# Delta rule and hard-swish MLP: the next step's product with the state moved into the run of the state update

## The chip, the cores and the metric

The kernel runs on one NeuronCore of a Trainium2 chip. A core has five engines that run side by side, each with its own queue of instructions: TensorE (PE, with its weight loads shown as PEld), VectorE (DVE), ScalarE (ACT), GpSimd (POOL) and SyncE (SP, which here only issues transfers). They wait for each other by semaphores. The metric is the device time of one execution in microseconds (us); less is better.

## The reference, cut to what matters

```python
batch, n_heads, seq, head_dim = (4, 8, 768, 48)
for t in range(S):
    kt, vt, bt = (k_n[:, :, t], v[:, :, t], beta[:, :, t, None])
    y[:, :, t] = np.einsum('bhd,bhde->bhe', q[:, :, t], state)
    v_old = np.einsum('bhde,bhd->bhe', state, kt)
    state = state + bt[:, :, :, None] * np.einsum('bhd,bhe->bhde', kt, vt - v_old)
...
h = x @ w_in
relu6 = np.clip(h + 3.0, 0.0, 6.0)
g = h * relu6 / 6.0
return (g @ w_out).astype(np.float32)
```

The first part is linear attention by the delta rule over 768 tokens for each of 4 x 8 heads of width 48; `k_n` are the keys divided by their norm. Its output, 3072 tokens by 384, goes through an MLP with 2048 hidden columns. All is float32.

## The kernel before

**Steps.** The 768 tokens are cut into 24 chunks of C = 32. One step t handles one chunk of all four batches and eight heads at once (4 x 32 = 128 partitions). Within a chunk the recurrence is turned into products of small matrices:

- `sc` (L547): keys times keys and queries times keys of the chunk, one 32x32 block a head. Masked and scaled by beta (L558) they become L, which is inverted, and LB.
- `X`: the inverse of the unit triangular matrix of L, made on VectorE for a group of four steps at a time (`inverse`, L759 and L764: 30 pairs of a product and a subtraction; L469 and L473 transpose into and out of the layout for it).
- `ks` (L806): keys and queries of the chunk times the state of the step before. Half of it, even and odd batches apart, gives R = V - K state (L901, L909); the other half starts the output y (ScalarE L843, VectorE L819).
- `pz` (L827): X R, copied by ScalarE to Z (L927).
- `su` (L938): the state's change, keys times Z, subtracted from the state by two VectorE operations of 128x384 (L956).
- `py` (L827): LB ("B") times Z, added to y (L863). y is then transposed on TensorE (`yt`, L873) and copied into the MLP's input `xT` (L877).

All of ks, pz, su, py and sc consist of 32 matmuls on 32- or 64-row tiles of TensorE (64 instructions each in the profile, as a float32 matmul is two). The keys and queries of a later step are transposed by four large matmuls each (`pt`, L524).

**MLP.** It works on blocks of two steps (256 tokens). From block 3 on the first product is formed by `up_by_eleven` (L1066: pairs `begin(j)`, `end(j)`; ScalarE copies, GpSimd adds L1030, VectorE L1093, L1097 and L1113 follow each end). From block 2 on the second product is formed by `down_by_seven` (L1226: seven products in two halves each, with sums of g on VectorE, L1212, ahead of some).

**Order.** The whole program is written out by hand; each engine runs its instructions in the program's order. The string ORDER gives the order up to step 4. From step LS = 5 on the main loop (L1469 and below) does it: each step has NU = 15 units, and in each unit one entry of `plan` is taken first (parts of the attention), then one unit of the MLP, then some of `fill` (VectorE's work on norms and inverses of a later group). `chain(t)`, `prep(t)` and `norms(g)` are generators; `take` runs one to its next `yield`. Before, `chain(t)` is taken in units 0 (ks), 1 and 2 (R), 3 (the y half), 4 (pz), 8 (su and py), 9 (y add and state update) and 10 (yt). A block's 14 half products down fall in units 13, 14 of an even step and 0 to 11 of the next; the 16 parts up follow.

**PSUM.** ks, su and sc share two pairs of banks (`ring("pc", 2, ...)`): ks and su take both pairs, sc one. The rest share four banks (`pm`).

**Fill.** `CHAIN` and `USED` are by unit and by form the time that VectorE is taken to be used by others; `due` spreads the inverse's 62 parts over what is left. The inverse of group g+1 starts at unit 6 of the second step of group g, and what is left is drained at unit 2 of the first step of group g+1.

Of the kernel before, what the change touches and what calls it, by code (L numbers as in the profile page):

```python
# [44 lines left out]
def kernel(  # L45
# [21 lines left out]
    nc = tc.nc  # L67
# [7 lines left out]
    GS = 4  # L75
# [696 lines left out]
        yield  # L772


    xTs, outs, zs = {}, {}, {}

    def banks(name, t, i):
        ring("pc", NPC, (name, t, i))
# [8 lines left out]
    def chain(t, whole=True):  # L787
# [7 lines left out]
            needs(("state", t - 1))  # L795
        bkb = bkb_of(t)

        def of_state():
            ph = [banks("ks", t, i) for i in range(2)]
            for p in range(NP):  # L800
                for b in (0, 2, 1, 3):
                    for e in range(2):
                        r = slice(DP * e, DP * e + DP)
                        c = slice(2 * C * (b // 2), 2 * C * (b // 2) + 2 * C)
                        y = b % 2
                        nc.tensor.matmul(  # L806
                            ph[y][c, e, D * p : D * p + D],
                            lhsT=KQ[r, p * B // 2 + b // 2, 2 * y : 2 * y + 2, :].rearrange(
                                "k y c -> k (y c)"
                            ),  # L810
                            rhs=state[r, b, p, :],
                            start=(p == 0), stop=True, skip_group_check=True,
                            tile_position=(DP * e, 2 * C * (b // 2)),
                        )
            return [pairs(x) for x in ph]
# [21 lines left out]
        def output(Z=None):  # L837

            if t > 0:
                needs(("turned", t - 1))  # L840
            y = work.tile([P, DM], FP32, name="y", bufs=1)
            if t > 0:
                nc.scalar.activation(  # L843
                    out=by_pair(y[:]), in_=even, func=ACTF.Copy, scale=parity[:, 1, 1:2]
                )
                past.add(("even", t))
                if ("R", t) in past:
                    read(("ks", t, 0))
                yield 1
                plus(y[:], odd, parity[:, 0, 1:2], y[:])  # L850
                read(*(("ks", t, i) for i in range(2)))
                yield
            needs(("Z", t))
            Z = zs.pop(t)
            ring("pm", NPM, ("py", t))
            py = psM.tile([P, 512], FP32, name="py", tag=slot["pm"])
            of_heads(py, lambda b: b ^ 1, lambda h: LB[:, he(h), :], Z)
            past.add(("BZ", t))
            yield
            if t == 0:  # L860
                nc.scalar.activation(out=y[:], in_=py[:, 0:DM], func=ACTF.Copy)
            else:
                nc.vector.tensor_tensor(out=y[:], in0=y[:], in1=py[:, 0:DM], op=ALU.add)  # L863
            read(("py", t))
            yield
            blk, cc = divmod(t, CB)
            if cc == 0:
                needs(*([("up", blk - 2)] if blk >= 2 else []))
                xTs[blk] = work.tile([128, NKT, TB], FP32, name="xT")
            ring("pm", NPM, ("yt", t))  # L870
            pt = psM.tile([128, NKT, P], FP32, name="yt", tag=slot["pm"])
            for s in range(NKT):
                nc.tensor.transpose(pt[:, s, :], y[:, s * 128 : (s + 1) * 128], ident[:])  # L873
            past.add(("turned", t))
            yield 1
            read(("yt", t))
            nc.scalar.activation(  # L877
                out=xTs[blk][:, :, cc * P : (cc + 1) * P], in_=pt[:], func=ACTF.Copy
            )
            past.add(("seam", t))  # L880
            yield
# [10 lines left out]
        if t == 0:  # L892
            R = vfl
        else:
            needs("parity")
            needs(("BZ", t - 1), ("su", t - 1))
            Rt = work.tile([P, DM], FP32, name="R", bufs=1)
            R = Rt[:]
            Rp = R.rearrange("p (e z) -> p e z", e=2)
            for e in range(2):  # L900
                nc.vector.scalar_tensor_tensor(  # L901
                    out=Rp[:, e].rearrange("p (a w) -> p a w", w=D), in0=even[:, e],
                    scalar=parity[:, 0, 0:1], in1=by_pair(vfl)[:, e], op0=ALU.mult, op1=ALU.add,
                )
            if ("even", t) in past:
                read(("ks", t, 0))
            if whole:
                yield
            nc.vector.scalar_tensor_tensor(  # L909
                out=Rp, in0=odd.rearrange("p e a w -> p e (a w)"), scalar=parity[:, 1, 0:1],  # L910
                in1=Rp, op0=ALU.mult, op1=ALU.add,
            )
            yield

        if whole and t > 0:
# [32 lines left out]
        past.add(("su", t))  # L948
        if whole:
            take(outs[t])  # L950
        yield
        if whole:
            take(outs[t])
        for i, x in enumerate(su):
            sv = state[:, 2 * i : 2 * i + 2].rearrange("p b a w -> p b (a w)")
            nc.vector.tensor_tensor(  # L956
# [2 lines left out]
        past.add(("state", t))  # L959
        read(*(("su", t, i) for i in range(B // 2)))  # L960
        yield
        if whole:
            take(outs[t])
            yield

# [395 lines left out]
    def chain_of(t):  # L1361
        return made(("h", t), lambda: chain(t))
# [53 lines left out]
        }  # L1416

    def behind_tensor(ins):
        last = next(
            i for i in reversed(nc.cur_bb.bb.instructions) if i.engine == mybir.EngineType.PE  # L1420
        )
        tc.add_manual_dep(
            ins, last.name,
            mybir.DependencyInfo(mybir.DependencyClass.Sync, mybir.DependencyReason.DATA),
            reason="held back",
        )

    def do(word):
        if word in ("K", "Q", "V", "W"):
# [22 lines left out]
    with tc.manual_schedule():  # L1452
# [11 lines left out]
        loads = iter(())  # L1464
        left = due = 0
        USED = {"up": 0.42, "eleven": 1.0, "down": 0.7}
        APART = (8, 12)
        CHAIN = {0: 0.45, 1: 0.75, 2: 0.75, 3: 0.4, 4: 0.4, 6: 0.5, 9: 0.8, 10: 0.6, 14: 0.2}
        for t in range(LS, N):  # L1469
            g, i = group(t)  # L1470
            ch = chain_of(t)
            behind = t == LS
            now, more, third, later = (prep_of(t + LA - n) for n in (2, 1, 0, -1))
            if not behind:
                now = third
            take(gens["v"], 4)
            if i == 0:
                left += 1
            if i == 2:
                loads = keys_of(g + 3)  # L1480
            plan = {
                0: lambda: take(ch),
                1: lambda: (take(ch), take(now)),
                2: lambda: (take(ch), take(now), take(gens["q"], 4)),
                3: lambda: take(ch),
                4: lambda: (take(ch), take(now, t not in APART)),
                5: lambda: take(now, t not in APART),
                6: lambda: take(now),
                7: lambda: take(now, t in APART),
                8: lambda: take(ch),  # L1490
                9: lambda: take(ch),
                10: lambda: take(ch),
                11: lambda: token_sums(t // CB),
                13: lambda: take(later),
            }
            if behind:
                plan[13] = None
                for u, gen in zip((3, 5, 5, 6, 7, 9, 10, 11, 12, 13), (more,) * 5 + (third,) * 5):
                    plan[u] = lambda old=plan.get(u), gen=gen: (old and old(), take(gen))
            ready = (1, 6)  # L1500
            for u in range(NU):
                if plan.get(u):
                    plan[u]()
                take(loads, 2)
                if (i, u) == (0, 2):
                    drain(fill)
                    left = 0
                    fill = norms_of(g + 2)
                if (i, u) == ready:
                    drain(fill)  # L1510
                    fill = inverse_of(g + 1)
                    take(fill)
                    left, due = 2 * (C - 2) + 2, 0.0
                take(rest)
                take(gens["a"])
                take(units)
                settle(1)
                while evicts:
                    evicts.pop(0)()
                if i == 1 == ready[0] and 5 < u < 7:  # L1520
                    continue
                if i == 0 or not left:
                    take(fill, 2 if i or u < 2 else u > 4)
                    continue
                room = max(1.65 - USED[mode["of"]] - CHAIN.get(u, 0), 0.15) / mode["mean"]
                due += room * left / max((GS - i) * NU - u, 1)
                due = min(due, 2.6)
                take(fill, int(due))
                left, due = max(left - int(due), 0), due - int(due)
            if behind:  # L1530
                take(later)
            drain(ch)
# [32 lines left out]
```

## Time and profile before

| | |
|---|---|
| time, median of 3 runs | 664.62 us (662.32 to 664.71) |
| span of the profiled execution, first to last instruction | 660.3 us |
| mean granted TensorE clock in it | 0.997 |
| L1066 PE, ph, busy | 156.8 us in 128x128 and 128x256 with `xT`, 55.9 with `beta_tok` |
| L1226 PE, po, busy | 110.6 + 86.7 us |
| L806 PE, ks | 26.9 us busy, 1472 instructions |
| L938 PE, su | 19.5 us busy, 1408 instructions |
| L1212 / L1113 DVE | 56.1 / 52.6 us busy |
| L759 / L764 DVE, inverse | 57.3 / 55.1 us busy, 150 each |

The time of a run is that of the whole execution; the span of the profiled one leaves out what lies ahead of the first and behind the last instruction. Busy times of small matmuls overlap on TensorE, so their sum is not time; what counts is from one's start to the next one's start.

### The profile page before, as it was taken

The page shows a single profiled execution, that of the slowest core. Times are in us where ns is not written, and L with a number is a line of the kernel's source. Part 1 is how long each engine was busy: PE and PEld are TensorE (multiplying, and loading weights), DVE is VectorE, ACT ScalarE, POOL GpSimd, SP SyncE. Part 2 cuts the span into 40 slices and gives each one's busy share as a digit, 9 for nine tenths or more (in the row PEclk, how much of TensorE's full clock was granted, in tenths as well). Part 3 has the DMA queues.
Part 4 walks back from the last instruction along what each step waited for, and adds up shares of the span by engine and source line. Part 5 has one row for each costly group of instructions (what it writes and reads, how often), then busy time and mean ns, then how long its engine had stood idle before and what let it go on. Part 6 is the DMA issues. An engine that isn't in the chain of part 4 may idle for free.

```text
span 660.3 us, 26640 instructions
## 1 busy us (share of the span) xinstructions
PE 632.5 (96%) x11640; PEld 569.2 (86%) x11640; DVE 499.2 (76%) x1170; ACT 282.3 (43%) x548; POOL 225.1 (34%) x352
## 2 busy tenths in 40 slices
PE   2768999999999999999999999999999999999997
PEld 2658987776689989999999999999999999999997
DVE  5899877798657988758988848979658998456354
ACT  5887689332243154154154244244244144153250
POOL 6531022003661353553254354164051242331430
PEclk9998999999999999999999999999999999999999
DMA  7888346202040030041030030020020020000000
GB/s 174 204 198 235 77 102 164 51 25 43 9 87 18 3 74 3 3 90 22 3 74 3 2 74 3 2 63 2 3 50 2 3 49 3 23 18 2 26 1 24
DMA packets 88692, 33.28 MB, mean 50 GB/s; under 512 B 80224, under 2 KB 83424, under 8 KB 88576
## 3 DMA queue, kind: packets, MB, share of 16 engines
q1 hardware_dynamic: 88224, 31.29, 20.8%
q8 instruction: 91, 1.49, 0.9%
q10 hardware_dynamic: 352, 0.30, 0.2%
q14 instruction: 25, 0.20, 0.1%
HBM read 26.84 MB, written 4.72 MB: 48 GB/s over the span
## 4 chain that ended last, share of the span: by engine, by line
PE 91%; DVE 3%; DMA 2%; SPq 1%; ACT 1%; issue 1%; DVEq 0%
PE po L1226 28%; PE ph L1066 27%; PE ph L994 9%; PE po L1162 6%; PE ks L806 4%; PE su L938 3%; PE pt L524 3%; PE pz L827 3%; PE py L827 3%; PE sc L547 2%; PE yt L873 1%; DMA spare<-in_moe_w_in_dram 1%; PE pi L684 1%; DMA w_out<-in_moe_w_in_dram 1%; SPq L168 1%
## 5 line engine op out<-in xcount | busy, mean ns | idle before, releaser
L1066 PE MATMUL ph<-xT,w_in 128*128 128x128 f32 (+1 forms) x720 | 156.8, 321 | 0.0
L1030 POOL TENSOR_TENSOR g<-g 128x256 f32<-128x256 f32 (+1 forms) x144 | 88.6, 616 | 104.7 <-ACT g L1080 99.1
L1066 PEld LDWEIGHTS ph<-xT,w_in 128*128 128x128 f32 x720 | 116.8, 191 | 6.7
L1226 PE MATMUL po<-w_out,g 128*128 128x192 f32 x640 | 110.6, 326 | 0.0
L1226 PEld LDWEIGHTS po<-w_out,g 128*128 128x128 f32 x640 | 104.6, 190 | 0.5
L1080 ACT ACTIVATE g<-ph 128x512 f32<-128x512 f32 x72 | 43.1, 598 | 105.1 <-PE ph L1066 105.1
L1226 PE MATMUL po<-spare,g 128*128 128x192 f32 x480 | 86.7, 332 | 0.0
L1226 PEld LDWEIGHTS po<-spare,g 128*128 128x128 f32 x480 | 77.2, 190 | 1.8
L994 PE MATMUL ph<-xT,w_in 128*128 128x128 f32 (+1 forms) x384 | 72.0, 338 | 0.6 <-ACT xT L877 0.6
L1236 POOL TENSOR_TENSOR o<-o,u 128x192 f32<-128x192 f32 x18 | 13.3, 739 | 163.8 <-ACT o L1233 86.6
L994 PEld LDWEIGHTS ph<-xT,w_in 128*128 128x128 f32 x384 | 59.6, 195 | 7.7 <-ACT xT L877 0.8
L1093 DVE TENSOR_TENSOR g<-ph,g 128x256 f32<-128x256 f32 x72 | 30.2, 419 | 46.8 <-PE ph L1066 33.5
L759 DVE TENSOR_TENSOR pr<-A 128x30 f32<-128x30 f32 (+9 forms) x150 | 57.3, 382 | 3.3
L1212 DVE TENSOR_TENSOR g<-g 128x512 f32<-128x512 f32 x80 | 56.1, 722 | 3.5 <-PE po L1226 3.5
L1113 DVE SCALAR_TENSOR_TENSOR g<-o,g 128x512 f32<-128x512 f32 x72 | 52.6, 730 | 7.8 <-ACT o L1110 7.7
L764 DVE TENSOR_TENSOR A<-A,pr 128x30 f32<-128x30 f32 (+9 forms) x150 | 55.1, 367 | 3.3
L1110 ACT ACTIVATE o<-g,halves 128x512 f32<-128x512 f32 x72 | 52.2, 725 | 11.3 <-DVE g L1113 8.4
L1066 PE MATMUL ph<-beta_tok,sums_in 128*128 128x128 f32 x288 | 55.9, 275 | 0.0
L356 ACT ACTIVATE spare<-spare,places 128x768 uint16<-128x768 uint16 (+1 forms) x56 | 52.8, 947 | 3.2 <-DMA kf<-in_k_dram 1.6
L1233 ACT ACTIVATE o<-po 128x192 f32<-128x192 f32 x40 | 13.3, 332 | 82.7 <-PE po L1226 79.2
L510 POOL TENSOR_TENSOR kb<-kf,inv 128x384 f32<-128x384 f32 x24 | 21.7, 907 | 75.5 <-issue 43.1
L1162 PE MATMUL po<-w_out,g 128*128 128x384 f32 x128 | 45.4, 490 | 0.0
(141 smaller groups left out, 1019.1 us busy)
## 6 DMA issues: line engine op xcount, KB each, us to landing
kf<-in_k_dram SPq DMA_DIRECT2D x96, 48.0 KB, 2.6
qb<-in_q_dram SPq DMA_DIRECT2D x96, 48.0 KB, 2.4
vf<-in_v_dram SPq DMA_DIRECT2D x96, 48.0 KB, 2.1
out_dram<-o SPq DMA_DIRECT2D x90, 48.0 KB, 1.6
spare<-in_moe_w_in_dram SPq DMA_DIRECT2D x4, 768.0 KB, 6.6
w_out<-in_moe_w_in_dram SPq DMA_DIRECT2D x4, 768.0 KB, 6.1
w_out<-in_moe_w_out_dram SPq DMA_DIRECT2D x4, 768.0 KB, 5.8
spare<-in_moe_w_out_dram SPq DMA_DIRECT2D x4, 768.0 KB, 5.2
```

The source lines that it names most:

```text
L356: nc.scalar.activation(out=z, in_=z if n else d.bitcast(I16)[:, :, :, 3], func=func, bias=places[:, n : n + 1], scale=scale,)
L759: nc.vector.tensor_tensor(out=pv, in0=A[:, j + 1 :, j].unsqueeze(2).to_broadcast([n, w, j]), in1=A[:, j, 0:j].unsqueeze(1).to_broadcast([n ...
L764: nc.vector.tensor_tensor(out=A[:, j + 1 :, 0:j], in0=A[:, j + 1 :, 0:j], in1=pv, op=ALU.subtract)
L994: nc.tensor.matmul(ph[:, cols], lhsT=w_in[:, s, f * 128 : (f + 1) * 128], rhs=xT[:, s, cols], start=(s == 0), stop=(s == NKT - 1),)
L1030: nc.gpsimd.tensor_tensor(out=out, in0=a, in1=b, op=op)
L1066: nc.tensor.matmul(ph[:, n], lhsT=w, rhs=x, start=start, stop=stop, skip_group_check=True)
L1080: nc.scalar.activation(out=gt, in_=ph[:], func=ACTF.Copy)
L1110: nc.scalar.activation(out=r, in_=g, func=ACTF.Relu, bias=half, scale=1.0 / 6.0)
L1113: nc.vector.scalar_tensor_tensor(out=g, in0=r, scalar=1.0, in1=g, op0=ALU.min, op1=ALU.mult)
L1162: nc.tensor.matmul(pos[c][:], lhsT=gs[blk, f // 2][:, f % 2, c * P : (c + 1) * P], rhs=w_out[:, f, :], start=(f == 0), stop=(f == NFC - 1),)
L1212: nc.vector.tensor_tensor(out=A(f, *out, 4), in0=A(f, *a, 4), in1=A(f, *b, 4), op=op)
L1226: nc.tensor.matmul(ps[n][:], lhsT=A(f - f % 2, *a)[:, f % 2], rhs=b[:, f], start=(f == 0), stop=(f == HF - 1),)
```

## The change

- In steps after LS = 5, ks uses one pair of banks instead of two: the two halves stand side by side in it.
- In these steps ks(t+1) is taken in step t: unit 8 takes su, py and the state update of step t, then `prep`'s sc, then ks of step t+1 (`nxt`). The scores' masks (L558) follow in unit 10.
- R of step t+1 is formed in units 12 and 13 of step t. In step t+1 the y half is taken in unit 1, pz in unit 5, su in 8, the y add in 9, yt in 10.
- The state update stands ahead of the y add in the program.
- ScalarE's read of ks for y (L843) is held behind the last operation that forms R (`held`).
- The inverse of the next group starts at unit 11 instead of 6 of a group's second step, is spread four units further, and is drained at unit 4 instead of 2 of the next group's first step. `CHAIN` is replaced.
- Step 5 keeps its own plan, with ks(6) in unit 12.

```diff
+    def held(ins, last):
+        tc.add_manual_dep(
+            ins, last.name,
+            mybir.DependencyInfo(mybir.DependencyClass.Sync, mybir.DependencyReason.DATA),
+            reason="held back",
+        )
...
+        apart = t <= LS
+
         def of_state():
-            ph = [banks("ks", t, i) for i in range(2)]
+            if apart:
+                ph = [banks("ks", t, i) for i in range(2)]
+            else:
+                both = banks("ks", t, 0)
+                w = NP * D
+                ph = [both[:, :, w * i : w * i + w] for i in range(2)]
...
-                            start=(p == 0), stop=True, skip_group_check=True,
+                            start=(p == 0 and (apart or y == 0)), stop=True,
+                            skip_group_check=True,
...
+                if not apart:
+                    needs(("R", t))
+                    held(nc.cur_bb.bb.instructions[-1], lasts[t])
                 past.add(("even", t))
-                if ("R", t) in past:
+                if ("R", t) in past and apart:
                     read(("ks", t, 0))
                 yield 1
                 plus(y[:], odd, parity[:, 0, 1:2], y[:])
-                read(*(("ks", t, i) for i in range(2)))
+                read(*(("ks", t, i) for i in range(2 if apart else 1)))
...
+            lasts[t] = nc.cur_bb.bb.instructions[-1]
             yield
...
         past.add(("su", t))
         if whole:
             take(outs[t])
-        yield
-        if whole:
-            take(outs[t])
+        else:
+            yield
         for i, x in enumerate(su):
...
         yield
-        if whole:
+        for _ in range(2 if whole else 0):
             take(outs[t])
             yield
...
-        APART = (8, 12)
-        CHAIN = {0: 0.45, 1: 0.75, 2: 0.75, 3: 0.4, 4: 0.4, 6: 0.5, 9: 0.8, 10: 0.6, 14: 0.2}
+        CHAIN = {
+            1: 0.6, 6: 0.2, 7: 0.9, 8: 0.9, 9: 0.45, 10: 0.6, 11: 0.3, 12: 0.6, 13: 0.5,
+        }
         for t in range(LS, N):
             g, i = group(t)
             ch = chain_of(t)
+            nxt = chain_of(t + 1) if t + 1 < N else iter(())
...
             plan = {
-                0: lambda: take(ch),
                 1: lambda: (take(ch), take(now)),
-                2: lambda: (take(ch), take(now), take(gens["q"], 4)),
-                3: lambda: take(ch),
-                4: lambda: (take(ch), take(now, t not in APART)),
-                5: lambda: take(now, t not in APART),
-                6: lambda: take(now),
-                7: lambda: take(now, t in APART),
-                8: lambda: take(ch),
+                2: lambda: (take(now), take(gens["q"], 4)),
+                5: lambda: take(ch),
+                8: lambda: (take(ch), take(now), take(nxt)),
                 9: lambda: take(ch),
-                10: lambda: take(ch),
+                10: lambda: (take(ch), take(now)),
                 11: lambda: token_sums(t // CB),
-                13: lambda: take(later),
+                12: lambda: take(nxt),
+                13: lambda: (take(nxt), take(later)),
             }
...
-            ready = (1, 6)
+            ready, due_by = (1, 11), 2 if behind else 4
...
-                if (i, u) == (0, 2):
+                if (i, u) == (0, due_by):
                     drain(fill)
...
-                if i == 1 == ready[0] and 5 < u < 7:
+                if (i, u) == ready:
                     continue
-                if i == 0 or not left:
-                    take(fill, 2 if i or u < 2 else u > 4)
+                if not left or behind:
+                    take(fill, 2 if i or behind and u < 2 else u > due_by + 2)
                     continue
...
-                due += room * left / max((GS - i) * NU - u, 1)
+                due += room * left / max((GS - i) % GS * NU - u + 4, 1)
```

## The prediction, made before the changed kernel ran

> Short names: a step is one pass t of the main loop, u0 to u14 its fifteen units. Odd steps from 7 on are down-steps (seven-product form, L1226), even ones from 8 on up-steps (eleven-product form, L1066). An island is a run of small tiled matmuls (ks, pz, sc, su, py) between large ones. n0 to n13 are the half products of the down form; n0 falls in u13 of the step before. Line numbers are those of the kernel before.
>
> **What bounds it.** First the page: the span, the busy shares, the chain that ended last, the clock.
>
> ```profile
> span 660.3 us, 26640 instructions
> PE 632.5 (96%) x11640; PEld 569.2 (86%) x11640; DVE 499.2 (76%) x1170; ACT 282.3 (43%) x548; POOL 225.1 (34%) x352
> ...
> PE 91%; DVE 3%; DMA 2%; SPq 1%; ACT 1%; issue 1%; DVEq 0%
> ```
>
> Then the sums over stretches of time:
>
> ```profile
> 190.00:590.00 400.00, 400.00 (x7220) 372.67 (x7222) 315.93 (x730) 146.64 (x305) 152.53 (x225) 1.00 0.13 26
> 49.50:66.00 16.50, 14.56 (x332) 13.45 (x333) 15.56 (x52) 12.33 (x25) 2.85 (x7) 0.90 0.82 235
> ```
>
> TensorE (first busy column) works 400.00 of 400.00 us between 190 and 590 us, at full clock; the list of waits has none on TensorE from 62 to 655 us. So a time saved on TensorE there is saved in full, and every wait put in front of it is paid in full. VectorE has only 84 us of slack in those 400, and it is in bursts.
>
> **What the islands cost.** TensorE's timeline in step 22:
>
> ```profile
> 587.85 1.03 PE L1066 MATMUL ph<-xT,w_in 128*128 128x256 f32 x4
> 588.81 0.89 PE L938 MATMUL su<-R,bkb 32*64 32x48 f32 x64
> 589.63 0.88 PE L827 MATMUL py<-R,LB 32*32 32x48 f32 x64
> 590.44 0.49 PE L1066 MATMUL ph<-xT,w_in 128*128 128x128 f32 x2
> 590.76 0.39 PE L1066 MATMUL ph<-beta_tok,sums_in 128*128 128x128 f32 x2
> ```
>
> Four large instructions of 0.216 pitch take 0.86; here 0.96 pass to su: 0.09 to 0.10 to enter. The first pair after py takes 0.32, not 0.22: 0.10 to leave. So an island costs 0.197 beyond its instructions. su's 64 starts take 0.816, py's 0.812, and pz is as long ahead of sc as alone: no price between kinds inside one. In the two programs' order of instructions TensorE has the same matmuls, and 89 islands before, 69 after: 17 of ks(7) to ks(23), and three of sc (steps 5, 8, 12). Saved: 20 x 0.197 = **3.9 us**. Inside an island ks was never seen beside others; its entry there costs between 0 and 0.1 x 17 = 1.7 us. I take 0, as between the other kinds.
>
> The Trainium skill ("TensorEngine Tiling (Array Packing)", Key Properties) says that a change of tiling mode drains TensorE. If each change of tile shape cost 0.1, a step's changes would fall only from 8 to 7 (7 to 6 without sc), and the saving would be about 2 us, the sum 684. The trace disagrees for su, py and pz, sc, whose shapes differ and whose pitch does not move.
>
> **The wait it adds inside the island.** Before, ks(t+1) stood seven units after su(t). Now su, py, (sc,) ks follow each other. ks needs the state update (L956, two VectorE operations); sc needs the PSUM pair that the first of them reads, and behind sc and ks all of TensorE waits. py covers 0.81 us, sc 0.79 more; sc exists up to step 17 only. So what matters is when VectorE starts the update. Its own queue in step 22:
>
> ```profile
> 588.99 0.42 DVE L1093 TENSOR_TENSOR g<-ph,g 128x256 f32<-128x256 f32 x1 [1.08 <-PE ph L1066]
> 589.45 0.29 DVE L1097 TENSOR_TENSOR g<-ph,g 128x128 f32<-128x128 f32 x1
> 589.66 0.68 DVE L1113 SCALAR_TENSOR_TENSOR g<-o,g 128x512 f32<-128x512 f32 x1
> 590.58 0.55 DVE L863 TENSOR_TENSOR y<-y,py 128x384 f32<-128x384 f32 x1 [0.24 <-PE py L827]
> 591.05 1.01 DVE L956 TENSOR_TENSOR state<-state,su 128x384 f32<-128x384 f32 x2
> ```
>
> In an up-step unit 7 ends a large group right ahead of su, and its three VectorE operations stand ahead of the update in both programs. L1093 cannot start until 0.18 after su's start (588.81), and L1113 gives VectorE up 0.60 after its start (as from 359.47 to 360.08 below), at 590.26. So the update starts s = 1.45 after su's start, its first half is done at s + 0.55, both at s + 1.01; VectorE to TensorE takes 0.05 (sums_in waits at 13 to 61 us). TensorE is there at 1.63. Waits: with sc s + 0.60 - 1.63, without sc s + 1.06 - 1.66 (two ks matmuls need only the first half).
> - Steps 10 and 14 (sc): 0.42 each. Steps 18, 22 (no sc): 0.85 each. Together 2.54.
> - Steps 8, 12, 16, 20 have inverse steps (L759, L764, 0.40 each at these sizes) in the queue: four between the last two ends, so 0.66 + 0.60 + 1.60 = 2.86 against TensorE's 2.43 (L1093 at 586.56 and at 588.99), late by 0.43; and one more ahead of the update. s = 2.28: 1.25 three times, 1.68 once: 5.4.
> - Down-steps: nothing of TensorE's newest work stands ahead; VectorE is free. The update starts 0.27 after su's last start, as L863 after py's (589.63 + 63 x 0.0127 = 590.31), so s = 1.07: 0.04 with sc (7 to 17; step 6 alike), 0.47 at 19 and 21: 1.2.
> Together **+9.2**. Lowest: every step as in a down-step, 2.8. Highest: VectorE as slow as where GpSimd runs beside it (L1113 1.00 instead of 0.68, about 0.9 a step in eight up-steps): 16.
>
> **The inverse moves too.** The diff spreads group g+1's inverse later: it must be drained by u4 instead of u2 of the group's first step, and X R moves from u4 to u5. Two units shrink to one between the last transpose (L473) and the matmul that needs it. VectorE before, step 13, and TensorE's two ends of that stretch:
>
> ```profile
> 359.47 0.69 DVE L1113 SCALAR_TENSOR_TENSOR g<-o,g 128x512 f32<-128x512 f32 x1 [0.85 <-ACT o L1110]
> 360.08 0.24 DVE L759 TENSOR_TENSOR pr<-A 128x84 f32<-128x84 f32 x1
> ...
> 361.53 0.09 DVE L768 MEMSET A<- 128x32 f32 x1
> 361.65 1.99 DVE L473 STREAM_TRANSPOSE X<-A 128x1024 f32<-128x1024 f32 x1
> ```
> ```profile
> 355.75 2.76 PE L1226 MATMUL po<-w_out,g 128*128 128x192 f32 x16
> ...
> 365.80 0.88 PE L827 MATMUL pz<-R,X 32*32 32x48 f32 x64
> ```
>
> VectorE leaves the last L1113 of the up form 4.33 after n0 starts (360.08 - 355.75), since L1113 waits for ScalarE and for the one before. Before, six inverse steps, the memset and the transpose follow: X is ready at 363.64, 2.2 ahead of pz. After, its queue holds there (same order in steps 9, 13, 17, 21): 14 inverse steps (13 in step 9) of 0.22 to 0.39, 4.1 together; L909, 0.52; two L819, 0.65; three L1212 of 0.60; memset 0.12; transpose 1.99. That is 9.2, less 0.4 where independent neighbours overlap: 8.8. X is ready at n0 + 13.1. pz stands behind seven half products of 1.30 and two pt of 0.44: n0 + 10.05 (ks's 1.28 is gone, one unit of 1.30 has come). Wait 3.05 + 0.05, four times: **+12.4**. Lowest: VectorE on time at the last end of the up form, 1.75 each, 7. Highest: with GpSimd's 0.9, 4.0 each, 16. Nothing queued on TensorE behind pz can pass it; VectorE catches up meanwhile, so su three units later is not late.
>
> **At nothing.** Computing R two units after ks and y even behind it: R is 7 units ahead of pz, hidden under 9 us of large matmuls. One PSUM pair instead of two for ks: both reads end at u1, su takes the pair at u8. The y add behind the update: yt comes two units later. Later LB: its reader is steps away. No DMA is added; values' loads stand at the same place.
>
> **The sum.** 660.3 - 3.9 + 9.2 + 12.4 = 678.0 us of span. The median of the runs, 664.62, is 4.3 above the profiled span; with it **682 us**.
>
> **Rivals.**
> 1. *Both waits* (682, 54%), own range 676 to 687.
> 2. *The clock falls as well* (12%). Between 49.5 and 66 us the granted clock is 0.90, 1.65 us lost, behind idle times of 2.41 and 0.58. A wait of 3.1 could do the same four times: 682 + 6.6 = 689. Against: one unbroken stretch of large matmuls surrounds each. The Trainium skill ("TensorE: Matmul & The Clock Gate", Part 1) states the rule: about 3.4 us of idle window and the clock is halved; the trace's one 3.4 us stretch at half clock agrees.
> 3. *X is in time, only the islands wait* (16%): 682 - 12.4 = 670. For: before it was 2.2 ahead. Against: eight more inverse steps and three sums stand ahead of it now.
> 4. *Only X waits* (8%): 673.
> 5. *Not slower* (10%): VectorE is never late. In u13 to u4 it would have to do 8.8 us of work in 5.7, and in up-steps start the update at su's end. From a total wait under 3.9 us on it is no loss; with none 664.62 - 3.9 = 660.7. For: VectorE is idle 1.0 to 1.4 us at many ends. Against: L1093 ahead of the update waits for TensorE itself.
> That the islands don't merge is excluded by the order of instructions.
>
> **The numbers.** Within 0.5% (3.3 us) is no change that this measurement can tell. Rival 5 splits into faster 5% and same 5%; the rest is slower, 90%. The range 668 to 691 holds cases 1 to 4 and their bounds but for the ends.
>
> **What would show it.** Right: waits on TensorE of sc and ks for the state update, 0.4 to 1.7 in up-steps, near 0 in down-steps up to 17; waits of pz for X near 3 in steps 9, 13, 17, 21 and no others; 0.2 less around each former ks. Wrong: TensorE still without gaps from 190 to 590 us, or the wait of pz at another step, for ScalarE's R, or none.

## The result, and the profile after

The changed kernel takes 729.42 us (median of 6 runs, 727.09 to 733.33), the kernel before 663.71 on the same chip (6 runs, 662.32 to 665.0): 1.0998 times as long, 95% interval 1.0972 to 1.1024. The profiled execution took 727.87, its span is 726.2: 65.9 more than before. Line numbers are now those of the changed kernel: ks L820, pz and py L842, su L957, the state update L974, y add L881, end of a large group L1084 followed by L1111, L1115 and L1131 on VectorE, half products L1244 with their sums L1230. sc (L547), X (L473) and the inverse (L759, L764) keep theirs.

The page of the changed kernel, its top and the chain of work that ended last:

```profile
span 726.2 us, 26601 instructions
PE 653.3 (90%) x11640; PEld 589.3 (81%) x11640; DVE 501.6 (69%) x1170; ACT 279.0 (38%) x548; POOL 225.8 (31%) x352
q8 instruction: 91, 1.49, 0.9%
PE 61%; DVE 26%; issue 5%; DMA 3%; ACT 2%; SPq 1%; POOL 1%; DVEq 0%; ACTq 0%; POOLq 0%
```

VectorE has 26% of the chain (3% before) and "issue", time in which the engine waited for nothing that the profile shows, 5%. The sums over stretches of time (columns: us, busy time of the five engines with counts, granted TensorE clock, DMA share, GB/s):

```profile
190.00:590.00 400.00, 362.94 (x6327) 339.22 (x6326) 279.52 (x635) 124.58 (x265) 135.47 (x201) 0.97 0.13 25
256.67:260.08 3.41, 3.41 (x62) 3.32 (x55) 0.00 (x0) 0.11 (x1) 0.00 (x0) 0.50 0.00 0
393.20:400.03 6.83, 5.28 (x76) 5.19 (x77) 4.17 (x6) 0.82 (x2) 0.83 (x1) 0.50 0.00 1
```

TensorE, never idle here before, misses 37 of 400 us and 893 of its 7220 instructions. The other two rows are stretches at half clock; there are eight such stretches, 37.5 us together, between 66 and 655 us, and there was none before the change. The list of TensorE's waits (total us, times, longest):

```profile
PE pz L842 <- DVE X L473: 15.4, 4, 4.0
PE sc L547 <- DVE state L974: 9.4, 7, 2.7
...
PE ks L820 <- issue: 7.3, 7, 1.6
PE sc L547 <- issue: 4.6, 3, 1.8
PE ks L820 <- DVE state L974: 3.6, 3, 2.9
...
PE ph L1084 <- issue: 1.2, 1, 1.2
PE pz L842 <- ACT g L1118: 1.1, 2, 0.8
```

The first, second and fifth line are the predicted waits. The three "issue" lines are not in the prediction. TensorE's timeline in step 10 shows both kinds in one island:

```profile
312.53 1.03 PE L1084 MATMUL ph<-xT,w_in 128*128 128x256 f32 x4
313.49 0.89 PE L957 MATMUL su<-R,bkb 32*64 32x48 f32 x64
314.31 0.88 PE L842 MATMUL py<-R,LB 32*32 32x48 f32 x64
315.53 0.86 PE L547 MATMUL sc<-KQ 64*32 64x64 f32 x64 [0.35 <-DVE state L974]
316.32 1.15 PE L820 MATMUL ks<-state,KQ 64*64 64x48 f32 x64
317.40 0.38 PE L1084 MATMUL ph<-xT,w_in 128*128 128x128 f32 x1
318.98 0.27 PE L1084 MATMUL ph<-xT,w_in 128*128 128x128 f32 x1 [1.20 <-issue]
```

sc starts 1.22 behind py, whose 64 starts take 0.81: a wait of 0.42, as predicted for step 10. The entry is 0.96 as before, and sc to ks takes 0.79. Behind ks and one large matmul TensorE stops for 1.20 us though no semaphore holds it.

Taken from start to start against the kernel before's pitches, the span's 65.9 us are: waits for X 15.65, waits for the state update 14.3, eleven stalls without a semaphore 15.5 (ten of them over 0.5), excess pitch in the half-clock stretches 16.2, islands saved -3.9. What is left, 8 us, is many small waits, the longest of them pz's 0.83 for ScalarE; it is not split further here.

**Where the stalls stand.** All instructions of TensorE (weight loads, matmuls and its recorded semaphore operations) are counted from the start of the trace. The ordinal of each matmul behind a stall of over 0.5 us in the changed kernel, divided by 256:

```
at us      201.8  230.0  290.8  319.0  344.7  406.0  434.2  462.1  523.8  548.1
ordinal     8129   9152  10945  11968  12737  14529  15552  16577  18369  19136
remainder    193    192    193    192    193    193    192    193    193    192
```

In the 13 traces of this case there are 68 such stalls behind 66 us, and all 68 have the remainder 192 or 193. So TensorE stops at the edges of blocks of 256 instructions. The page's queue q8 brings instructions: 91 packets, 1.49 MB, or 16 KB each, as many as TensorE has blocks. In all 68 cases TensorE resumes 1.20 to 1.57 us after the end of the latest of these packets, 2.2 to 2.9 after its start: it waited for its instructions. The blocks ahead of the stalls lasted 3.45 us (median), the stall included. In the kernel before, a block of large matmuls alone (at 621 us) takes 17 us; 128 pairs of weight load and matmul of an island take 1.6 to 2.2.

Nearly every stall follows a block that lies wholly among small matmuls, but not every such block is followed by one. Behind 66 us the 13 traces have 123 such blocks; packets and blocks are matched here by their numbers.

| small instructions right ahead of the block | blocks | packet for the block behind it starts | followed by a stall over 0.5 us |
|---|---|---|---|
| 41 or more | 72 | in 71 behind the block's first edge, by up to 1.6 us | 58; in 13 of the others TensorE waited 0.8 us or more for a semaphore inside the block |
| fewer | 51 | in 46 ahead of that edge, by up to 3.0 us | none of these 46; 4 of the other 5 |

So what tells the two apart is whether the packet starts ahead of the edge, and that goes with what stands in the 40 instructions or so ahead of it. The kernel before has three such blocks, at 190, 397 and 566 us, with packets 2.0, 0.9 and 3.0 us ahead of the edge and no stall: its islands, of at most 128 pairs from step 6 on, hold a whole block only by an exact fit, with large matmuls right ahead. The merged island is 256 pairs up to step 17, which always hold one, and 192 behind, which may.

The Trainium skill ("Runtime: NRT & Kernel Launch", Instruction fetch mechanics) states blocks of 16 KiB or 256 instructions, which these traces agree with, and that crossing an edge is mostly hidden; here it is hidden behind large matmuls and costs 0.6 to 2.3 us where an island runs into a stall.

### The profile page after: what moved, and what is told of

Read it like the earlier page. It is cut to its first block, busy times and chain, and to the rows that moved or that the text cites. A ratio compares the mean times of both kernels' runs of the same rounds, so it can differ in the third digit from the quotient of the medians.

```text
span 726.2 us, 26601 instructions
## 1 busy us (share of the span) xinstructions
PE 653.3 (90%) x11640; PEld 589.3 (81%) x11640; DVE 501.6 (69%) x1170; ACT 279.0 (38%) x548; POOL 225.8 (31%) x352
## 3 DMA queue, kind: packets, MB, share of 16 engines
q8 instruction: 91, 1.49, 0.9%
## 4 chain that ended last, share of the span: by engine, by line
PE 61%; DVE 26%; issue 5%; DMA 3%; ACT 2%; SPq 1%; POOL 1%; DVEq 0%; ACTq 0%; POOLq 0%
PE po L1244 17%; PE ph L1084 15%; PE ph L1012 8%; PE po L1180 6%; DVE g L1131 4%; DVE A L764 4%; PE ks L820 4%; DVE pr L759 4%; PE pz L842 2%; DVE g L1230 2%; DVE g L1111 2%; PE sc L547 2%; PE pt L524 2%; PE su L957 2%; DVE g L1115 2%
## 5 line engine op out<-in xcount | busy, mean ns | idle before, releaser
L1084 PE MATMUL ph<-xT,w_in 128*128 128x128 f32 (+1 forms) x720 | 155.8, 324 | 1.7 <-issue 1.2
L1048 POOL TENSOR_TENSOR g<-g 128x256 f32<-128x256 f32 (+1 forms) x144 | 91.4, 636 | 125.3 <-ACT g L1098 119.3
L1084 PEld LDWEIGHTS ph<-xT,w_in 128*128 128x128 f32 x720 | 120.5, 195 | 8.0 <-issue 0.6
L1244 PE MATMUL po<-w_out,g 128*128 128x192 f32 x640 | 111.9, 329 | 0.0
L1244 PEld LDWEIGHTS po<-w_out,g 128*128 128x128 f32 x640 | 106.3, 193 | 0.5
L1244 PE MATMUL po<-spare,g 128*128 128x192 f32 x480 | 94.5, 347 | 1.1 <-DVE g L1131 0.6
L1244 PEld LDWEIGHTS po<-spare,g 128*128 128x128 f32 x480 | 82.9, 201 | 4.8 <-DVE g L1131 2.0
L1111 DVE TENSOR_TENSOR g<-ph,g 128x256 f32<-128x256 f32 x72 | 30.1, 419 | 71.9 <-PE ph L1084 71.8
L1254 POOL TENSOR_TENSOR o<-o,u 128x192 f32<-128x192 f32 x18 | 13.7, 763 | 177.1 <-DVE u L1254 102.4
L1012 PEld LDWEIGHTS ph<-xT,w_in 128*128 128x128 f32 x384 | 59.6, 194 | 8.4 <-ACT xT L895 0.8
L764 DVE TENSOR_TENSOR A<-A,pr 128x30 f32<-128x30 f32 (+9 forms) x150 | 59.5, 397 | 3.3
L1131 DVE SCALAR_TENSOR_TENSOR g<-o,g 128x512 f32<-128x512 f32 x72 | 54.2, 753 | 8.7 <-ACT o L1128 8.7
L759 DVE TENSOR_TENSOR pr<-A 128x30 f32<-128x30 f32 (+9 forms) x150 | 57.6, 384 | 3.1
L1084 PE MATMUL ph<-beta_tok,sums_in 128*128 128x128 f32 x288 | 57.3, 281 | 0.3 <-DVE beta_tok L1074 0.3
L1230 DVE TENSOR_TENSOR g<-g 128x512 f32<-128x512 f32 x80 | 54.1, 700 | 1.5 <-PE po L1244 1.5
L1084 PEld LDWEIGHTS ph<-beta_tok,sums_in 128*128 128x128 f32 x288 | 45.2, 198 | 1.7 <-issue 1.3
```

The source lines that it names most:

```text
L759: nc.vector.tensor_tensor(out=pv, in0=A[:, j + 1 :, j].unsqueeze(2).to_broadcast([n, w, j]), in1=A[:, j, 0:j].unsqueeze(1).to_broadcast([n ...
L764: nc.vector.tensor_tensor(out=A[:, j + 1 :, 0:j], in0=A[:, j + 1 :, 0:j], in1=pv, op=ALU.subtract)
L1012: nc.tensor.matmul(ph[:, cols], lhsT=w_in[:, s, f * 128 : (f + 1) * 128], rhs=xT[:, s, cols], start=(s == 0), stop=(s == NKT - 1),)
L1048: nc.gpsimd.tensor_tensor(out=out, in0=a, in1=b, op=op)
L1084: nc.tensor.matmul(ph[:, n], lhsT=w, rhs=x, start=start, stop=stop, skip_group_check=True)
L1111: nc.vector.tensor_tensor(out=gt[:, 1:3], in0=ph[:, 1:3], in1=gt[:, 3].unsqueeze(1).to_broadcast([128, 2, P]), op=ALU.add,)
```

## The experiments

All but the fourth, seventh, eighth and ninth start from the changed kernel. Times are medians of 4 runs beside 663.5 to 663.7 of the kernel before.

### 1. sc and ks as an island of their own

```diff
-                8: lambda: (take(ch), take(now), take(nxt)),
+                8: lambda: take(ch),
...
-                10: lambda: (take(ch), take(now)),
-                11: lambda: token_sums(t // CB),
+                10: lambda: (take(ch), take(now), take(nxt)),
+                11: lambda: (token_sums(t // CB), take(now)),
```

> The changed kernel, but sc and ks of the next step are issued two units behind su and py, as an island of their own, so that no island has more than 128 pairs of weight load and matmul; X and its wait stay as in the changed kernel. Theory (four separate costs: waits for the state update 14.3 us, waits for X 15.65, stalls of TensorE with no semaphore behind them in the islands of 192 and 256 pairs 15 to 16, and some 17 us by half-clock stretches that follow the longest of these): the waits of sc and ks for the state update and the stalls marked issue in the middle of islands are gone, the four waits of pz for X stay near 4 us each, the half-clock stretches behind the X waits stay (9 to 10 us lost), 17 islands more cost 3.4. 729.4 - 14.3 - 15.5 - 7.5 + 3.4 = 695 us (690 to 701). Rival (the stalls marked issue have nothing to do with the length of the island but with the slow clock or with GpSimd and VectorE being late): they stay, and only the state waits and their clock loss go: about 711 us (706 to 716).

697.14 us, ratio 1.0508 (1.0467 to 1.0549). Its list of TensorE's waits:

```profile
PE pz L842 <- DVE X L473: 14.8, 4, 4.0
...
PE yt L891 <- DVE y L881: 4.9, 4, 1.7
```

No line names the state update any more. This is inside the theory's range. Two stalls of over 0.5 us at block edges, both at other edges, stand against ten: the same instructions, in islands of at most 128 pairs, run through. New is yt waiting for the y add in steps 8, 12, 16 and 20.

### 2. X in time

```diff
-            ready, due_by = (1, 11), 2 if behind else 4
+            ready, due_by = (1, 11), 2 if behind else 0
...
-                due += room * left / max((GS - i) % GS * NU - u + 4, 1)
+                due += room * left / max((GS - i) % GS * NU - u, 1)
```

> The changed kernel, but the inverse of the next group is drained at the start of the group's first step (due at unit 0 instead of unit 4); the merged islands stay. Theory: the four waits of pz for X (15.65 us in all) go to nearly nothing, and with them the half-clock stretches behind them (20.5 of the 37.5 us at half clock, 9 to 10 us lost); state waits and issue stalls in the islands stay: 729.4 - 15.7 - 9.5 = 704 us (700 to 710). Rival (X is late because VectorE is short of time, not because of the due time): the wait moves to the two ends of the up form at units 10 to 14 or to the state update, and the kernel gains less than 8 us: above 721.

719.41 us, 1.0849 (1.0787 to 1.091): 10 us gained, of 25 expected. Its waits:

```profile
PE po L1244 <- DVE g L1230: 9.7, 4, 2.5
PE sc L547 <- DVE state L974: 9.4, 7, 2.7
```

pz waits for X no more, but in the same four steps a half product waits 2.5 us for its sum, which now stands behind the inverse in VectorE's queue. That is what the rival said, though the gain is a little over its bound. The half-clock stretches did not shrink (34.1 us instead of 37.5).

### 3. Both

Both diffs together.

> Both edits in one: inverse drained at unit 0 of the group's first step, and sc with ks of the next step as an island two units behind su and py. What is left of the change is X R alone, R and y even behind ks, one PSUM pair for ks, and sc moved to ks. Theory (the four costs are all there is): as many islands as before but for the three lone sc: 663.7 - 0.6 plus 0 to 3 us of small waits = 663 to 666 us, with no TensorE wait over 0.5 us between 62 and 655 us and full clock. Rival (something of the rest costs too: the one PSUM pair, R and y, the later LB): above 670, with its waits on TensorE named.

687.19 us, 1.036 (1.0305 to 1.0414): the rival's side. Its waits:

```profile
PE po L1244 <- DVE g L1230: 9.5, 4, 2.4
...
PE yt L891 <- DVE y L881: 6.7, 4, 1.9
```

From start to start they are 10.1 and 7.4; with 2.1 at half clock, 19.6 of the 23.5 us. No stall at a block edge and no wait for state or X is left. So with the later start of the inverse VectorE is late in the four up-steps 8, 12, 16, 20 or at the start of the steps behind them at both ends that were tried.

### 4 and 7. Longer islands in the kernel before

```diff
-            of_heads(py, lambda b: b ^ 1, lambda h: LB[:, he(h), :], Z)
+            for _ in range(3 if t > LS else 1):
+                of_heads(py, lambda b: b ^ 1, lambda h: LB[:, he(h), :], Z)
```

The seventh has 2 in place of 3.

> The kernel before, with the 64 matmuls of py issued three times over into the same PSUM pair, the same values each time, from step seven on: the island of su and py grows from 128 to 256 pairs of weight load and matmul, while nothing is waited for that was not waited for before. Theory (TensorE's instructions are brought by transfers of 16 KB, 256 instructions or 128 pairs each, that come no faster than one in about 3.5 us, while an island of 256 pairs runs through two of them in 3.4): beside 17 x 2 x 0.812 = 27.6 us of matmuls, one stall of 0.5 to 2.0 us marked issue in nearly every island of 256 pairs, 10 to 25 us in all: 663.7 + 27.6 + 15 = 706 us (701 to 716). Rival (the stalls came from the state, the PSUM pair or the queue order of the changed kernel): no such stalls, 691 us (689 to 694).

> The kernel before with py issued twice from step seven on, the same values each time: islands of su and py of 192 pairs. Theory (instruction supply): 17 x 0.812 = 13.8 us of matmuls, and stalls marked issue in some of the islands, shorter than in those of 256 pairs: 0.3 to 0.9 each, 3 to 12 us in all: 685 us (680 to 690). Rival (a threshold: 192 pairs pass without a stall): 677.5 us (676 to 679).

Three times: 722.73 us, 1.0904 (1.0855 to 1.0953). Twice: 687.01, 1.0344 (1.031 to 1.0379). Three times, the first line from the list of waits, then the timeline of step 10 (su, py and ph stand at L939, L827 and L1067 in this kernel):

```profile
PE py L827 <- issue: 20.5, 12, 2.2
```
```profile
312.82 0.55 PE L939 MATMUL su<-R,bkb 32*64 32x48 f32 x31
313.30 1.55 PE L827 MATMUL py<-R,LB 32*32 32x48 f32 x125
316.51 0.95 PE L827 MATMUL py<-R,LB 32*32 32x48 f32 x67 [1.67 <-issue]
317.39 0.49 PE L1067 MATMUL ph<-xT,w_in 128*128 128x128 f32 x2
```

Nothing is waited for that was not before, and yet TensorE stops amid py's own matmuls, at remainder 192 or 193 all 14 times. There are 18 steps with added py, not 17: 18 x 1.624 = 29.2 us of matmuls, 27.5 of stalls, 3.1 at half clock, against 59.0 measured. The time lies above the theory's 701 to 716, as most stalls are longer than expected, 1.5 to 2.3 us. With 192 pairs, inside the theory's range, there are four stalls, of 1.5 to 2.3 us: whether such an island holds a whole block depends on where the edges fall.

### 5 and 6. sc and the inverse back in their old place

The fifth is the third with sc beside X R in unit 5, its mask in unit 6, and the inverse from unit 6 to unit 2 again; the sixth is the same with ks right behind su and py (islands of 192 pairs).

```diff
-                5: lambda: take(ch),
-                8: lambda: (take(ch), take(now), take(nxt)),
+                5: lambda: (take(ch), take(now)),
+                6: lambda: take(now),
+                8: lambda: take(ch),
...
+                10: lambda: (take(ch), take(nxt)),
...
-            ready, due_by = (1, 11), 2 if behind else 4
+            ready, due_by = (1, 6), 2
...
```

> As the third experiment (both edits), but sc and the mask of a later step go back to units 5 and 6 (sc beside X R) and the inverse of the next group back to its start at unit 6 of the group's second step and its end at unit 2 of the next group's first, as in the kernel before. Left of the change: X R one unit later and apart from su, R and y behind ks, one PSUM pair for ks. Theory (the 23 us that the third experiment kept come from the inverse's later start: VectorE gets the same work squeezed into the up-steps 8, 12, 16 and 20): the waits of po for L1230 (9.5 us) and of yt for y (9.1) are gone, 663.7 us (661 to 667). Rival (R and y behind ks, or the one PSUM pair, make VectorE late in up-steps whatever the inverse does): the waits of yt for y stay, 672 us or more.

> As the fifth, but ks of the next step stands right behind su and py again, as in the changed kernel: islands of 192 pairs, sc beside X R, inverse as in the kernel before. Theory (state wait and instruction supply are costs of their own): X in time; ks waits for the state update 0.4 to 0.5 in down-steps, 0.85 in steps 10, 14, 18, 22, and no more than 1.7 in 8, 12, 16, 20 because the inverse is no longer squeezed into them: 11 to 14 us; stalls marked issue of 0.5 to 0.9 in islands of 192 pairs, 5 to 12 us; 3.9 saved on islands: 683 us (675 to 691). Rival (the state waits of 2.75 to 2.95 in steps 8, 12, 16 and 20 come from the merged order itself): they stay, with the half-clock stretches behind them, 695 us or more.

678.51 us, 1.0245 (1.0202 to 1.0289), and 706.46, 1.0655 (1.0616 to 1.0693): both times on the rivals' side. A line of the fifth's waits, then one of the sixth's:

```profile
PE su L957 <- DVE LB L558: 5.1, 3, 1.7
```
```profile
PE ks L820 <- DVE state L974: 13.1, 12, 2.7
```

In the fifth (profiled execution 683.58 us) the waits for L1230 are gone as said, and of those of yt for y 2.3 us are left of 7.4. But su waits for sc's mask (it takes the pair of banks that the mask still reads) 1.9 us, from start to start, in steps 8, 12 and 16, X is 0.3 to 0.95 late, and there are two stalls of 1.8 us at block edges and 13.7 us at half clock. Both stalls are in islands of 128 pairs: one is the exact fit that the kernel before passes at 397 us, but with the packet 1.0 us behind the edge instead of 0.9 ahead; in the other the packet started 5.3 us behind the edge, behind a wait for X. These waits are of the arrangement, so the pair does not say what R and y behind ks cost by themselves; that stays open. In the sixth the state waits did not all stay, as its rival had it: in steps 8, 12 and 16, where su itself is held by the mask, they fell to 1.2 to 1.4 us, as the theory said, while steps 10 and 14 have 2.1. In step 20, where no sc is left to disturb, ks still waits 2.76: with the inverse no longer squeezed this was too long, and it led to the eleventh.

### 8 and 9. The inverse's part of the change alone, in the kernel before

```diff
-            ready = (1, 6)
+            ready = (1, 11)
...
```

That is the ninth. The eighth also puts X R at unit 5, spreads the inverse four units further and drains it at unit 4, as the change does.

> The kernel before with one part of the change alone: the inverse of the next group starts at unit 11 instead of 6 of the group's second step, is spread to end at unit 4 instead of 2 of the next group's first, and X R stands at unit 5 instead of 4 (sc stays at 4, an island of its own then: 9 x 0.2 = 1.8 us). ks, su and py, R and y stay where they were. Theory (the waits for X belong to the inverse's later place alone): pz waits for X in steps 9, 13, 17 and 21, 2.5 to 4 us each, 10 to 16 in all, half-clock stretches behind them 3 to 9: 663.7 + 1.8 + 13 + 6 = 685 us (678 to 692). Rival (X is late only because R and y stand late in VectorE's queue, behind ks of the same stretch): X in time, 666 us.

> The kernel before with the inverse's start alone moved from unit 6 to unit 11 of the group's second step; it still ends at unit 2, and X R stays at unit 4. Theory (VectorE has no room in the up-steps 8, 12, 16, 20 and the two steps after for what is moved into them): TensorE waits for X or for a sum of L1212 in steps 9, 13, 17, 21, some 2 to 4 us each with a half-clock stretch behind some: 677 us (670 to 688). Rival (five units out of 41 are spread thin enough): 664 us.

Eighth: 683.09 us, 1.0294 (1.0275 to 1.0313). Ninth: 672.35, 1.0131 (1.0105 to 1.0157). The eighth's waits, then the ninth's:

```profile
PE pz L827 <- DVE X L473: 8.9, 4, 2.6
```
```profile
PE pz L827 <- DVE X L473: 4.9, 4, 1.3
```

Both times are in the theories' ranges, with waits in the steps named, but these are mostly shorter than expected. The waits for X need no merged island: the later inverse makes them by itself, 1.3 us each by its start alone and 1.8 to 2.6 by start and end. In the changed kernel they are 3.6 to 4.1, and still 3.6 to 4.1 in the first experiment; which of the change's other parts adds the rest was not run alone. The ninth has no half-clock stretch behind 66 us, the eighth two.

### 10. The island one unit later

su, py, sc and ks in unit 9; the y add, yt with the masks and the token sums one unit later; R stays in units 12 and 13; the inverse from unit 12.

> The changed kernel with the island su, py, sc, ks at unit 9 instead of 8, and what follows one unit later. In up-steps unit 7 ends a large group and unit 8 begins one, so the three VectorE operations of that end run 1.2 us further ahead of the update. Theory (the state wait is set by what stands ahead of the update in VectorE's queue): the waits in steps 8, 12, 16 and 20 fall from 2.75 to 2.95 to some 1.6, those in 10, 14, 18 and 22 to nothing, those of down-steps stay; state waits 14.3 to about 8, two to four half-clock stretches of 3.41 fewer; the waits for X (one unit less of time for the inverse) grow by up to 1 each; issue stalls stay: 721 us (715 to 727). Rival (the update takes this long after su whatever stands ahead of it): state waits unchanged, 729 us or more.

757.02 us, 1.1381 (1.1333 to 1.143): the time was missed by far, since new waits came: large groups wait for L1074 behind yt, 14.1 us, and yt for y, 10.0. Of its waits (profiled execution 763.31 us):

```profile
PE ph L1084 <- DVE beta_tok L1074: 14.1, 9, 2.4
PE yt L891 <- DVE y L881: 10.0, 8, 1.5
PE sc L547 <- DVE state L974: 8.3, 3, 2.8
...
PE ks L820 <- DVE state L974: 2.8, 1, 2.8
```

The waits for the state update are gone in steps 10, 14, 18 and 22, as the theory said, and nearly so in the down-steps, where it had them stay. In 8, 12, 16 and 20, which it was about, they stay at 2.8, as the rival said. There VectorE's queue holds four of the inverse's operations between the last two ends ahead of the update: they filled the unit that was won.

### 11. No piece of the inverse shortly ahead of the update

```diff
+                if i == 3 and u in (5, 6, 7):
+                    continue
                 room = max(1.65 - USED[mode["of"]] - CHAIN.get(u, 0), 0.15) / mode["mean"]
```

> The changed kernel, but in the up-steps 8, 12, 16 and 20 no piece of the inverse is issued in units 5 to 7, so that nothing of it stands in VectorE's queue shortly ahead of the state update; the pieces are spread over the units behind. Theory (in these four steps the state wait is long because VectorE is still busy with the inverse's pieces): the waits fall from 2.75 to 2.95 to what steps 10, 14 and 18 show, 0.4 with sc and 0.8 without, 9 us less, with the half-clock stretches behind them; the waits for X grow by 1 to 2.5 each, since the same pieces are still to be done: 724 us (717 to 731). Rival (the order of the island sets these waits, whatever VectorE does before): they stay at 2.7 to 2.9, 729 us or more.

727.7 us, 1.0945 (1.0877 to 1.1012). Its waits:

```profile
PE pz L842 <- DVE X L473: 20.8, 4, 5.5
...
PE sc L547 <- DVE state L974: 3.9, 7, 0.9
...
PE ks L820 <- DVE state L974: 1.8, 3, 1.1
```

In steps 8, 12 and 16 the state wait fell from 2.75 to 0.95, in step 20 from 2.95 to 1.5, not all the way to 0.4 and 0.8; the waits for X grew by 1.2 to 1.4 each; and in steps 8, 12 and 16, where the wait had given the instructions time to come, stalls at block edges of 0.3 to 1.0 appeared. The waits went the theory's way; three costs changed, and the time did not clearly (727.7 against 729.42).

No run came below the kernel before. TensorE has no gap in it from 62 to 655 us, and the islands, 3.9 us at most, are all that the change could win.

## Why the prediction was wrong

It had the direction and both waits, but the range ended at 691. By its own steps:

- **The bound**: right. Each wait was paid in full.
- **What the islands cost**: right as far as it goes. Entry, pitches and the change of kinds inside cost what was said (0.96, 0.79 to 0.82, nothing). What this step did not ask is how long an island may get. In the kernel before none was over 128 pairs from step 6 on, so no row there shows a stall. This **missing term** is 15.5 us. Experiments 1, 4 and 7 and the ordinals show it.
- **The wait inside the island**: mechanism right, 14.3 us instead of 9.2. Steps 10 and 14 came out at 0.42 each as predicted, 18 and 22 at 0.77 for 0.85. Down-steps 11 and 15 have 0.37 for 0.04. The **mis-sized term** is steps 8, 12, 16 and 20: 2.75 to 2.95 instead of 1.25 to 1.68. VectorE in step 12 of the changed kernel:

```profile
365.57 0.42 DVE L1111 TENSOR_TENSOR g<-ph,g 128x256 f32<-128x256 f32 x1
366.02 0.29 DVE L1115 TENSOR_TENSOR g<-ph,g 128x128 f32<-128x128 f32 x1
366.23 0.97 DVE L1131 SCALAR_TENSOR_TENSOR g<-o,g 128x512 f32<-128x512 f32 x1
367.13 0.65 DVE L764 TENSOR_TENSOR A<-A,pr 128x228 f32<-128x228 f32 x1
367.81 0.39 DVE L759 TENSOR_TENSOR pr<-A 128x220 f32<-128x220 f32 x1
368.23 0.39 DVE L764 TENSOR_TENSOR A<-A,pr 128x220 f32<-128x220 f32 x1
368.65 0.38 DVE L759 TENSOR_TENSOR pr<-A 128x210 f32<-128x210 f32 x1
368.95 0.42 DVE L1111 TENSOR_TENSOR g<-ph,g 128x256 f32<-128x256 f32 x1
...
370.50 1.01 DVE L974 TENSOR_TENSOR state<-state,su 128x384 f32<-128x384 f32 x2
```

  su started at 366.69, so the last L1111 could have run at 366.87; it ran 2.08 later. I had it late by 0.43, from the one pair of ends shown. It was 1.1 late already at the end before (365.57, and TensorE's ends are 2.43 apart), and with GpSimd beside it L1131 takes 0.97 and L764 0.65. A queue that is filled to its brim carries its lateness from one end to the next. Experiment 11 takes the pieces out and the wait falls to 0.95 (1.5 in step 20).
- **The inverse moves too**: right. 15.65 instead of 12.4, inside the bounds of 7 to 16, in the four steps named. From the end of the last L1131 to X ready 9.6 us pass, not 8.8, as GpSimd runs beside it at 390 us. Experiments 8 and 9 show that the later inverse alone makes 1.8 to 2.6 us of each wait; the rest, up to 4.1, comes with the other parts of the change and stays open.
- **At nothing**: held in the changed kernel, but only under other waits. With these gone (experiments 1 and 3) the y add made yt wait 5 to 7 us.
- **Rival 2, the clock** (12%, 6.6 us): this is the **step that failed** beside the missing term. The clock fell and cost 16.2 us. "One unbroken stretch of large matmuls surrounds each" was no reason against it, as the next section's table shows; and not only X's waits did it: four of the eight half-clock stretches follow these, three follow a wait for the state, one a stall. The prediction took the one such stretch of the kernel before, at 51.80 us, as agreeing with some 3.4 us of idle time; the 3.41 us ahead of it held 2.1.

Without the missing term and the clock the same sum would have come to 682 + 5.1 + 3.2 = 690. The two add 31.7 us, and the small waits that were not split the rest, up to 729.

## What to carry to other kernels

Before small matmuls are joined into one run, count their instructions and not only their time: in this kernel runs of 128 pairs of weight load and matmul nearly always passed, and runs of 256 mostly met a block of instructions that had not come yet. A wait that is added to an engine without gaps can cost more than its length where it reaches a couple of microseconds, since the clock can fall behind it. And where another engine's queue is already filled up by a planner, moving one wait out of the way only brings the next one up: look at what the full engine has to do in that stretch, not at the one instruction that is late.

## What the runs showed of the hardware

**The clock falls behind steps of 3.41 us with enough idle time.** The half-clock stretches of a run begin on one raster of 3.413 us and last one or two steps. For all 12 changed runs, behind 66 us and up to some 5 us from the end, the steps at full clock by TensorE's idle time in them, and how many were followed by half clock:

```
idle in the step, us    below 1.0   1.0-1.25  1.25-1.5  1.5-1.75  1.75-2.0  2.0 and more
steps                        2011         28        20        28        24            29
then half clock                 0          1         2        12        16            29
```

So no wholly idle step is needed. Between 1.25 and 2.0 us the clock fell in 30 cases of 72, so the idle time as it is counted here does not settle it alone. A wait of 4 us always leaves 2.0 in some step; one of 2.75 may or may not. X's first wait in the changed kernel ends at 280.21 and fills 3.07 us of the step that ends at 280.56; half clock follows to 283.97. The Trainium skill ("TensorE: Matmul & The Clock Gate", Part 1) gives the same 3413 ns window but puts the fall behind an idle one; here 1.2 to 2.0 of its 3.41 us were enough.

**TensorE can outrun its own instructions**, as the section on the result shows: 68 stalls of 68 at an edge of a block of 256. Not shown is what sets the start of a packet. Five of the 68 stalls followed blocks of 4.0 to 7.7 us, longer than the usual 3.4; in the two longest the packet had started 5.0 and 5.3 us behind the edge.
